# A recurrence in front of two feed-forward layers: the first chunk's instructions written in another order

## The chip, the cores and the metric

The kernel runs on one core of a Trainium2 chip. The metric is the device time of one execution in microseconds (us), the median of three timed runs. One further execution was recorded by the profiler; all rows of the profile below are from that one. TensorE is called PE (its weight loads PEld), VectorE DVE, ScalarE ACT, GpSimd POOL, and SyncE SP.

## The reference

The input has 4 batches, 8 heads, 768 tokens and a head width of 40. A gated recurrence runs over the tokens; its result goes through two gated feed-forward layers.

```python
# recurrence, per batch, head and token t
m_new = max(f + m, i)
C = exp(f + m - m_new) * C + exp(i - m_new) * outer(v, k)
n = exp(f + m - m_new) * n + exp(i - m_new) * k
y = sigmoid(o) * (C @ q) / max(|n . q|, 1)
# first layer, 320 -> 1536 -> 320
x = (sigmoid(x @ w_gate) * (x @ w_val)) @ w_out
# second layer, 320 -> 2048 -> 320
h = x @ w_in
x = (h * clip(h + 3, 0, 6) / 6) @ w_out2
```

The weights of both layers arrive as 64-bit floats; the rest is float32.

## The kernel before, in words

Tokens are cut into six chunks of 128 (`c` = 0 to 5). Inside a chunk the recurrence is written as products, batch by batch (`b` = 0 to 3), in named pieces:

- `spread` and `decays`: the forget factors of a batch are spread over all partitions by PE and scanned by DVE (L405), in two halves. For batches 2 and 3 the factors come from memory (`dec_load`).
- `scores`: q times k on PE (L379), into two PSUM banks; `weigh`: DVE multiplies each bank by the decays (L420).
- `value_ones`, `values`, `values_end`: v scaled by the input gate (`vi`) and by the last decay (`vd`), on DVE (L370) or, if "apart", as eight ACT multiplies (L368).
- `outputs`: weighed scores times `vi` on PE (L474), in pieces of 32 tokens; then the products for the state (L497), in pieces of 32 columns. For c > 0 there is also the product with the state of the chunk before (L463).
- `denominators` (L521 to L525), `gated` (y, yo: L370, L533, L540), `out_gate` (the sigmoid of o, L426, in place in the tile `vko`), `state` (ACT copies of the state, L560 and L563).
- `att2`: yo is transposed by PE (L569); ACT copies the high part of the result (L574) and DVE the low part (L575) into x.

A first-layer weight tile `raw` (three buffers) is read by ACT twice (`scaled`, L102 and L107, into `u` with one buffer and `bits` with two), joined by DVE (`to_f32`, L122), and split into a high part by ACT (`hi_in`, `hi_out1`) and a low part by DVE (`lo_in`, `lo_out1`). A job is one such tile, in the order w1 of f = 0, w1 of f = 1, wo1 of both, and so on; `work(n, ...)` takes n jobs.

The first layer of chunk c is, for each of 12 blocks f: 16 products of 512 columns (`h_pair`, L587 to L594), the sigmoid (L613), the gate multiply (L614) and the split of the result into gh and gl (L600, L601) in `m1_h`; then eight products into three banks `acc` (`m1_out`, L629 and L639), two steps later.

What sets the order: everything up to the last weight conversion of chunk 0 stands in a block under `manual_schedule`, where each engine takes its instructions in the written order. The later steps are laid out by a scheduler, steered by `quota`, `issue_after` and the calls of `work`. Each engine works through its own row in order. DMAs go out on SP's queue, also in order; a fetch of a raw tile waits there until ACT has read the tile that held the buffer.

`later_factors` makes the factors of chunks 1 to 5: a scan on DVE (L311), five small multiplies (L320), transposes (L294) and one small product (L324) on PE into three banks of the same pool `acc` that the output products use, and three ACT copies (L298 twice, L331).

Of the kernel before, what the change touches and what calls it, by code (L numbers as in the profile page):

```python
# [8 lines left out]
F32 = mybir.dt.float32  # L9
# [24 lines left out]
def mlstm_then_two_gated_ffn(  # L34
# [27 lines left out]
    def ps_acc():  # L62
        return acc_ps.tile([P, 512], F32, tag="acc", name="acc")
# [242 lines left out]
        nc.vector.memset(fz[:, 1:, 0:1], 0.0)  # L306
        nc.sync.dma_start(out=fz_dram[1:].rearrange("c r l -> r c l"), in_=fz[:, 1:, :])

    def later_factors():

        nc.vector.tensor_tensor_scan(  # L311
            out=g_sb[:, L:S], data0=fz_sb[:, L:S], data1=fs_sb[:, L:S],
            initial=0.0, op0=ALU.mult, op1=ALU.add,
        )
        transpose_rows(i_c, iT, range(1, NC), ps_acc)
        transpose_rows(g, gT, range(1, NC), ps_acc)

        ge = const.tile([BH, NC, BH // 2], F32, name="ge")
        for c in range(1, NC):
            nc.vector.tensor_scalar(  # L320
                out=ge[:, c, :], in0=sel, scalar1=g[:, c, L - 1 : L], scalar2=None, op0=ALU.mult
            )
        ps = ps_acc()
        nc.tensor.matmul(  # L324
            out=ps[:, BH // 2 : NC * BH // 2],
            lhsT=par,
            rhs=ge[:, 1:, :].rearrange("p c n -> p (c n)"),
            start=True,
            stop=True,
        )  # L330
        nc.scalar.copy(  # L331
            out=gend[:, 1:].rearrange("p c b n o -> p (c b n o)"),
            in_=ps[:, BH // 2 : NC * BH // 2],
        )

    exp_half = const.tile([P, 1], F32, name="exp_half")
    sel = const.tile([BH, BH // 2], F32, name="sel")
    odd = const.tile([BH, 2, 1], F32, name="odd")
# [105 lines left out]
    def att1(c, b, ps):  # L444

        outputs(c, b, ps)
        with tc.issue_after(last_exp[-1]):
            out_gate(c, b)
        y = denominators(c, b, state if c > 0 else None)
        gated(c, b, y, c == 1 and b < 2)  # L450
        if c == 0:
            state(c, b)

    def outputs(c, b, ps):
        a = at[c, b]
        dec, vi = a["dec"], a["vi"]

        halves = [slice(t, t + 32) for t in range(0, L, 32)]
        if c > 0:
            o_ps = a["o_ps"] = ps()  # L460
            for n in range(NP):
                for tt in halves:
                    nc.tensor.matmul(  # L463
                        out=o_ps[tt, n * 2 * D1 : (n + 1) * 2 * D1],
                        lhsT=a["qk"][:, 0, n, tt],
                        rhs=cst[:, b, n, :],
                        start=n == 0,
                        stop=n == NP - 1,
                        skip_group_check=True,
                    )  # L470
        i_ps = a["i_ps"] = ps()
        for h in range(H):
            for tt in halves:
                own = nc.tensor.matmul(  # L474
                    out=i_ps[tt, h * D1 : (h + 1) * D1],
                    lhsT=dec[:, h, tt],
                    rhs=vi[:, h, :],
                    start=h == 0,
                    stop=h == H - 1,
                    skip_group_check=True,  # L480
                )
        if c < NC - 1:
            k_on = a["vko"].rearrange("p a n -> p (a n)")[:, DM:]
            beside = c > 0
            if beside:
                c_ps = i_ps[:, H * D1 : H * D1 + NP * D1]
            else:
                c_ps = (ps() if ps is any_ps else ps_mm())[:, : NP * D1]
            c_banks[c, b] = c_ps
            with ExitStack() as queued:  # L490
                if beside:
                    queued.enter_context(tc.issue_after(own.ins))
                for h in range(H):
                    p0 = 64 * (h % 2)

                    for d in (0, 32):
                        nc.tensor.matmul(  # L497
                            out=c_ps[p0 + d : p0 + d + 32, (h // 2) * D1 : (h // 2 + 1) * D1],
                            lhsT=k_on[:, h * D + d : h * D + d + 32],
                            rhs=a["vd"][:, h, :],  # L500
                            start=not beside and h < 2,
                            stop=h >= H - 2,
                            skip_group_check=True,
                        )
# [100 lines left out]
    gs = {}  # L605
    acc1 = {}

    def m1_h(c, f, ts):
        n = ts.stop - ts.start
        banks = [ps_mm()[:, :n], ps_mm()[:, :n]]  # L610
        h_pair(slots["in", f], (1, c), banks, ts)
        g = gpool.tile([P, T], F32, tag="g", name="g")[:, :n]
        gate = nc.scalar.activation(out=g, in_=banks[0], func=AF.Sigmoid).ins  # L613
        mult = nc.vector.tensor_tensor(out=g, in0=g, in1=banks[1], op=ALU.mult).ins  # L614
        gs[c, f, ts.start] = split_g(g)
        return gate, mult

    def m1_out(c, f, ts):
        if f == 0 and ts.start == 0:
# [102 lines left out]
    with tc.manual_schedule():  # L722
        nc.sync.dma_start(out=f_sb[:, :S], in_=gates[:, 0])
        nc.scalar.dma_start(out=i_sb[:, :S], in_=gates[:, 1])
        constants()
        for b in range(2):
            qk_load(0, b)
            vko_load(0, b)
        raws = [fetch(jobs[-1][0])]
        stabilise_first()  # L730
        nc.scalar.dma_start(out=fz_dram[0], in_=fz[:, 0, :])
        for b in range(2, B):
            qk_load(0, b)
# [12 lines left out]
        value_ones(0, 0)  # L746
        next(later)
        decays(0, 0, 1)
        values(0, 0, False)
        next(second)  # L750
        scores(0, 0, any_ps)
        values_end(0, 0, True)
        decays(0, 1, 0)
        next(later)
        weigh(0, 0, 0)
        weigh(0, 0, 1)
        next(second)
        decays(0, 1, 1)
        outputs(0, 0, any_ps)
        value_ones(0, 1)  # L760
        for b in range(2):
            out_gate(0, b)
        values(0, 1, False)
        values_end(0, 1, True)
        scores(0, 1, any_ps)
        y0 = denominators(0, 0)
        gated(0, 0, y0, False)
        decays(0, 2, 0)
        weigh(0, 1, 0)
        weigh(0, 1, 1)  # L770
        outputs(0, 1, any_ps)
        state(0, 0)
        decays(0, 2, 1)
        later_decays()
        value_ones(0, 2)
        values(0, 2, False)
        y1 = denominators(0, 1)
        att2(0, 0, any_ps)
        values_end(0, 2, True)
        scores(0, 2, any_ps)  # L780
        gated(0, 1, y1, False)
        decays(0, 3, 0)
        weigh(0, 2, 0)
        weigh(0, 2, 1)
        att2(0, 1, any_ps)
        decays(0, 3, 1)
        outputs(0, 2, any_ps)
        value_ones(0, 3)
        values(0, 3, False)
        values_end(0, 3, True)  # L790
        out_gate(0, 2)
        scores(0, 3, any_ps)
        y2 = denominators(0, 2)
        u = scaled(raws[0])
        weigh(0, 3, 0)
        weigh(0, 3, 1)
        outputs(0, 3, any_ps)
        gated(0, 2, y2, False)
        out_gate(0, 3)
        x0 = to_f32(raws[0], u)  # L800
        w0 = hi_in(jobs.pop()[2], x0)
        att2(0, 2, any_ps)
        y3 = denominators(0, 3)
        gated(0, 3, y3, False)
        lo_in(w0, x0)
        opened = att2(0, 3, any_ps)
        u = scaled(raws[1])
        x1 = to_f32(raws[1], u)
        w1_ = hi_in(jobs.pop()[2], x1)
        lo_in(w1_, x1)  # L810
        for b in range(1, B):
            state(0, b)
        u = scaled(raws[2])
        x2_ = to_f32(raws[2], u)
        wo_ = hi_out1(jobs.pop()[2], x2_)
        lo_out1(wo_, x2_)

    for b in range(2):
        att_load(1, b)
        dec_load(1, b)  # L820

    halves = (0, 6)

# [93 lines left out]
    for i, (c, f, ts) in enumerate(steps):  # L917
        for _ in range(quota[i]):
            for cp, b, piece in pieces.pop(0) if pieces else ():
# [7 lines left out]
                if cp > 0 and piece == 1 and nxt[0] < NC:  # L927
# [1 line left out]
                    dec_load(*nxt)  # L929
                    qk_load(*nxt)  # L930
                    vko_load(*nxt)
        gate = m1_h(c, f, ts)
        if i == 0:
            with tc.issue_after(gate[0]), tc.issue_after(gate[1]):
                later_factors()
        outputs_but(2 if i < n_two else 1)
        before.append((c, f, ts))
        if c == 0:
            work(1 + i % 2, n_w1)
        elif c < NC - 1:  # L940

            with tc.issue_after(gate[0]):
# [198 lines left out]
```

## Time and profile before

| | us |
|---|---|
| median of three runs | 846.74 (846.21 to 846.82) |
| profiled execution | 850.12 |
| its span | 848.30 |
| PE busy in it | 825.5 (97%) |
| DVE busy | 554.2 (65%) |
| ACT busy | 424.5 (50%) |

Busy time is that of one engine alone; matmuls are pipelined, so that a record's length is longer than the distance from one start to the next. A timeline row gives start and length, and in brackets how long the engine stood idle before it and what ended that. The windows give the granted clock of TensorE: 1.00 is 2.4 GHz, 0.50 is 1.2 GHz.

### The profile page before, as it was taken

The numbers are of one execution on the slowest core, as the hardware profiler recorded it, in microseconds if no ns is written. First come the engines' busy times: TensorE is split into PE (matmuls) and PEld (weight loads), VectorE is DVE, ScalarE is ACT, GpSimd is POOL, SyncE is SP. The second block draws the span as 40 slices with busy tenths as digits, with TensorE's granted clock in tenths as the row PEclk, the third lists the DMA queues.
The fourth block names the chain that finished last, engine by engine and source line by source line (L and its number), as shares of the span: only waits on it lengthen the run. The fifth ranks groups of instructions, "written<-read, shape, count | busy, mean of one in ns | idle before, by whom it ended". The sixth has DMA issues, their size and how long they took to land.

```text
span 848.3 us, 17178 instructions
## 1 busy us (share of the span) xinstructions
PE 825.5 (97%) x7013; PEld 706.5 (83%) x7013; DVE 554.2 (65%) x995; ACT 424.5 (50%) x851; POOL 2.5 (0%) x8
## 2 busy tenths in 40 slices
PE   6789999999999999999999999999999999999998
PEld 6567889988888878888888888888998889988898
DVE  8668885875867677766755534667746577466653
ACT  5488964332534344444323535556545555365542
POOL 1000000000000000000000000000000000000000
PEclk9679999999999999999999999999999999999999
DMA  9536644332565576567404524446625466244400
GB/s 338 190 124 222 210 155 149 119 104 74 155 223 175 175 218 200 170 198 212 130 25 138 167 78 156 143 131 205 182 77 168 148 198 178 79 130 141 121 32 32
DMA packets 81423, 128.69 MB, mean 152 GB/s; under 512 B 20672, under 2 KB 57472, under 8 KB 81344
## 3 DMA queue, kind: packets, MB, share of 16 engines
q1 hardware_dynamic: 81248, 127.48, 48.9%
q8 instruction: 55, 0.90, 0.4%
q14 instruction: 24, 0.20, 0.1%
q10 hardware_dynamic: 96, 0.11, 0.0%
HBM read 104.27 MB, written 23.30 MB: 150 GB/s over the span
## 4 chain that ended last, share of the span: by engine, by line
PE 91%; DVE 5%; ACT 2%; issue 1%; DMA 0%; DVEq 0%; ACTq 0%
PE acc L629 12%; PE mm L967 9%; PE mm L591 7%; PE mm L592 7%; PE mm L593 7%; PE mm L587 5%; PE att L967 4%; PE acc L967 4%; PE acc L639 4%; PE mm L594 4%; PE att L379 3%; PE mm L1004 2%; PE mm L1006 2%; PE acc L1004 2%; PE mm L1005 2%; PE acc L1006 2%
## 5 line engine op out<-in xcount | busy, mean ns | idle before, releaser
L600 ACT CAST gh<-g 128x512 fp32r<-128x512 f32 (+1 forms) x126 | 75.7, 601 | 101.6 <-DVE g L614 71.4
L591 PE MATMUL mm<-x,w 128*128 128x512 f32 (+1 forms) x312 | 118.0, 378 | 0.0
L592 PE MATMUL mm<-x,w 128*128 128x512 f32 (+1 forms) x312 | 117.7, 377 | 0.0
L593 PE MATMUL mm<-x,w 128*128 128x512 f32 (+1 forms) x312 | 117.5, 376 | 0.0
L601 DVE TENSOR_TENSOR gl<-g,gh 128x512 fp32r<-128x512 f32 (+1 forms) x126 | 83.5, 663 | 49.8 <-ACT gh L600 49.0
L614 DVE TENSOR_TENSOR g<-g,mm 128x512 f32<-128x512 f32 (+1 forms) x78 | 50.2, 644 | 84.6 <-PE mm L594 84.1
L629 PE MATMUL acc<-gh,w 128*128 128x512 f32 (+1 forms) x312 | 103.5, 376 | 0.0
L613 ACT ACTIVATE g<-mm 128x512 f32<-128x512 f32 (+1 forms) x78 | 43.9, 563 | 93.8 <-PE mm L594 93.7
L967 PE MATMUL mm<-X,wg 128*128 128x512 f32 x336 | 84.2, 392 | 0.0
L967 PEld LDWEIGHTS mm<-X,wg 128*128 128x128 f32 x336 | 61.9, 188 | 12.8 <-DVE g L983 0.3
L592 PEld LDWEIGHTS mm<-x,w 128*128 128x128 f32 x312 | 59.4, 191 | 11.2
L593 PEld LDWEIGHTS mm<-x,w 128*128 128x128 f32 x312 | 59.4, 190 | 11.1
L629 PEld LDWEIGHTS acc<-gh,w 128*128 128x128 f32 x312 | 58.5, 190 | 10.8 <-issue 0.2
L591 PEld LDWEIGHTS mm<-x,w 128*128 128x128 f32 x312 | 59.5, 191 | 9.5
L587 PE MATMUL mm<-x,w 128*128 128x512 f32 (+1 forms) x156 | 63.9, 410 | 2.9 <-DVE w L155 1.7
L629 PE MATMUL acc<-gl,w 128*128 128x512 f32 (+1 forms) x156 | 58.8, 377 | 0.0
L982 ACT ACTIVATE gb<-c,half 128x512 f32<-128x512 f32 x48 | 34.6, 724 | 48.2 <-DVE c L978 48.2
L594 PE MATMUL mm<-x,w 128*128 128x512 f32 (+1 forms) x156 | 58.7, 376 | 0.0
L601 DVE TENSOR_TENSOR gl<-gb,gh 128x512 fp32r<-128x512 f32 x48 | 33.0, 690 | 33.8 <-ACT gh L600 33.8
L600 ACT CAST gh<-gb 128x512 fp32r<-128x512 f32 x48 | 29.5, 620 | 39.4 <-PE att L1005 39.4
L405 DVE TENSOR_TENSOR_SCAN dec<-dec,ident 128x512 f32<-128x512 f32 x40 | 47.3, 1211 | 0.0
L967 PE MATMUL att<-X,wg 128*128 128x512 f32 x168 | 46.3, 395 | 0.0
(205 smaller groups left out, 1687.3 us busy)
## 6 DMA issues: line engine op xcount, KB each, us to landing
wg<-ws_dram SPq DMA_DIRECT2D x24, 896.0 KB, 5.3
raw<-in_w SPq DMA_DIRECT2D x20, 640.0 KB, 5.3
qk<-in_qkT SPq DMA_DIRECT2D x22, 512.0 KB, 4.6
wg<-wt_dram SPq DMA_DIRECT2D x48, 224.0 KB, 6.0
vko<-in_vko SPq DMA_DIRECT2D x22, 480.0 KB, 6.3
dec<-fz_dram SPq DMA_DIRECT2D x20, 512.0 KB, 5.0
raw<-in_wo SPq DMA_DIRECT2D x14, 640.0 KB, 3.9
X<-xt_dram SPq DMA_DIRECT2D x84, 64.0 KB, 3.1
```

The lines of the kernel that those rows point to most:

```text
L405: nc.vector.tensor_tensor_scan(out=x, data0=a["factors"][n] if "factors" in a else x, data1=ident4.rearrange("p h l -> p (h l)"), initial= ...
L587: nc.tensor.matmul(out=banks[j], lhsT=tail, rhs=xl[:, 2, :], start=True, stop=False)
L591: nc.tensor.matmul(out=banks[j], lhsT=hi, rhs=xh[:, k, :], start=False, stop=False)
L592: nc.tensor.matmul(out=banks[j], lhsT=hi, rhs=xl[:, k, :], start=False, stop=False)
L593: nc.tensor.matmul(out=banks[j], lhsT=lo, rhs=xh[:, k, :], start=False, stop=False)
L594: nc.tensor.matmul(out=banks[j], lhsT=tail, rhs=xh[:, 2, :], start=False, stop=True)
L600: nc.scalar.copy(out=gh, in_=g)
L601: nc.vector.tensor_tensor(out=gl, in0=g, in1=gh.bitcast(F32), op=ALU.subtract)
L613: gate = nc.scalar.activation(out=g, in_=banks[0], func=AF.Sigmoid).ins
L614: mult = nc.vector.tensor_tensor(out=g, in0=g, in1=banks[1], op=ALU.mult).ins
L629: nc.tensor.matmul(out=a[m], lhsT=lhsT, rhs=rhs, start=st and lhsT is hi and rhs is gh, stop=en and lhsT is lo, skip_group_check=True,)
L967: nc.tensor.matmul(out=ps, lhsT=w[:, a, s, :], rhs=x[:, b, :], start=first and i == 0, stop=i == 3, skip_group_check=True,)
```

## The change

The pieces of the recurrence of chunk 0 are written in another order, and some work is moved into that block:

- Raw weights are read by ACT earlier (`scaled(raws[0])` ahead of `outputs(0, 0)`, `scaled(raws[1])` after `att2(0, 1)`), with the fetch of the next raw tile, and the loads of chunk 1 (`att_tiles`, `qk_load`, `vko_load`, `dec_load`), called right behind.
- The sigmoids of batches 2 and 3 and the state copies of batches 1 to 3 stand earlier; `decays(0, 2, 1)` and `later_decays` stand ahead of `weigh(0, 1)`; `scores(0, 3)` ahead of `outputs(0, 2)`; `values_end(0, 3)` goes from ACT to DVE.
- For c = 0, `outputs` takes all 128 tokens in one product per head, and its state products 64 columns.
- Two h blocks (f = 0 and 1) and their gates are written in the block. `later_factors` is cut in three (`later_scan`, `later_ends`, the rest), placed around them.
- For chunk 1, `gated` of batches 0 and 1 scales y on DVE, no longer on ACT.
- `work(1 + i % 2)` becomes `work(2 - i % 2)`.

PE in the block, from the work of batch 1 up to the first h block. `dec`, `early` are decays, `vi`, `vd` scaled values, `yo` the gated output, `x` and `w` the operands of the first layer. Before:

```order
L569 MATMUL acc<-ident_81,yo 128x128 x3
L379 MATMUL att<-early 128x128 x8
L569 MATMUL mm<-ident_81,yo 128x128 x3
L474 MATMUL mm<-vi,early 32x41 x32
L497 MATMUL mm<-vd,early 32x41 x16
L379 MATMUL acc<-early 128x128 x8
L474 MATMUL acc<-vi,early 32x41 x32
L497 MATMUL att<-vd,early 32x41 x16
L569 MATMUL att<-ident_81,yo 128x128 x3
L294 MATMUL acc<-ident_81,early 128x32 x5
L379 MATMUL att<-qk 128x128 x4
L569 MATMUL mm<-ident_81,yo 128x128 x3
```

The change:

```order
L504 MATMUL acc<-vd,vko 64x41 x8
L384 MATMUL att<-early 128x128 x8
L576 MATMUL mm<-ident_81,yo 128x128 x3
L384 MATMUL mm<-early 128x128 x8
L480 MATMUL acc<-vi,early 128x41 x8
L504 MATMUL acc<-vd,early 64x41 x8
L480 MATMUL acc<-vi,early 128x41 x8
L504 MATMUL att<-vd,early 64x41 x8
L576 MATMUL att<-ident_81,yo 128x128 x3
L576 MATMUL mm<-ident_81,yo 128x128 x3
L384 MATMUL att<-qk 128x128 x7
```

`scores` of batch 3 (the second 128x128 x8) goes ahead of `outputs` of batch 2, the pieces become 8 products each, the transposes of `later_factors` (128x32) leave this place, and most scores of chunk 1 (`att<-qk`) stand behind both transposes of yo.

DVE, from y of batch 2 to the low part of x that h0 waits for (`den`: denominators, `bits`: a joined weight, L151 and L155 the low part of the first weight). Before:

```order
L370 TENSOR_TENSOR y<-mm,den 128x8x40
L533 TENSOR_TENSOR yo<-y,early 128x320
L122 SCALAR_TENSOR_TENSOR bits<-u,bits 128x640
L575 TENSOR_TENSOR x<-att,x 128x3x128
L521 TENSOR_SCALAR den<-acc 128x8
L524 TENSOR_TENSOR den<-den,acc 128x8
L525 RECIPROCAL den<-den 128x8
L370 TENSOR_TENSOR y<-acc,den 128x8x40
L533 TENSOR_TENSOR yo<-y,early 128x320
L151 TENSOR_TENSOR w<-bits,w 128x2x256
L155 TENSOR_TENSOR w<-bits,w 64x128 x2
L575 TENSOR_TENSOR x<-mm,x 128x3x128
```

The change:

```order
L375 TENSOR_TENSOR y<-acc,den 128x8x40
L540 TENSOR_TENSOR yo<-y,early 128x320
L528 TENSOR_SCALAR den<-acc 128x8
L531 TENSOR_TENSOR den<-den,acc 128x8
L532 RECIPROCAL den<-den 128x8
L375 TENSOR_TENSOR y<-acc,den 128x8x40
L540 TENSOR_TENSOR yo<-y,early 128x320
L582 TENSOR_TENSOR x<-att,x 128x3x128
L151 TENSOR_TENSOR w<-bits,w 128x2x256
L155 TENSOR_TENSOR w<-bits,w 64x128 x2
L582 TENSOR_TENSOR x<-mm,x 128x3x128
```

The joined weight (L122) is gone from here, it stands further up; the denominators of batch 3 stand ahead of the low part of x of batch 2.

ACT around the first two gates (`g`, `gh`; `cst` are the state copies, `iT`, `gT`, `gend` the factors of later chunks). Before:

```order
L560 COPY cst_86<-acc 104x164
L613 ACTIVATE g<-mm 128x512
L563 COPY cst<-cst_86 40x4x41 x2
L560 COPY cst_86<-mm 104x164
L298 COPY iT<-acc 128x160
L563 COPY cst<-cst_86 40x4x41 x2
L560 COPY cst_86<-att 104x164
L600 CAST gh<-g 128x512
L563 COPY cst<-cst_86 40x4x41 x2
L102 ACTIVATE u<-raw 128x640
```

The change:

```order
L624 ACTIVATE g<-mm 128x512
L102 ACTIVATE u<-raw 128x640
L107 ACTIVATE bits<-raw 128x640 x2
L607 CAST gh<-g 128x512
L165 CAST w<-bits 128x2x320
L624 ACTIVATE g<-mm 128x512
L102 ACTIVATE u<-raw 128x640
L607 CAST gh<-g 128x512
L298 COPY iT<-acc 128x160
L298 COPY gT<-acc 128x160
L335 COPY gend<-acc 128x80
```

The state copies are gone from between the gates; a weight's high part (L165) stands between gh of f = 0 and the second sigmoid, and the three copies of `later_factors` stand behind gh of f = 1.

The diff, cut to its core:

```diff
-        gated(c, b, y, c == 1 and b < 2)
+        gated(c, b, y, False)
...
-        halves = [slice(t, t + 32) for t in range(0, L, 32)]
+        m = 32 if c > 0 else L
+        halves = [slice(t, t + m) for t in range(0, L, m)]
...
-                    for d in (0, 32):
+                    m = 32 if beside else 64
+                    for d in range(0, 64, m):
...
         decays(0, 1, 1)
+        u0 = scaled(raws[0])
+        fetched.append(fetch(jobs[-4][0]))
+        att_tiles(1, 0)
+        qk_load(1, 0)
         outputs(0, 0, any_ps)
...
         gated(0, 0, y0, False)
+        vko_load(1, 0)
         decays(0, 2, 0)
+        decays(0, 2, 1)
+        later_decays()
         weigh(0, 1, 0)
         weigh(0, 1, 1)
+        att_tiles(1, 1)
+        qk_load(1, 1)
+        state(0, 0)
+        att2(0, 0, any_ps)
         outputs(0, 1, any_ps)
-        state(0, 0)
-        decays(0, 2, 1)
-        later_decays()
         value_ones(0, 2)
+        for b in range(2, B):
+            out_gate(0, b)
...
+        x0 = to_f32(raws[0], u0)
+        y1 = denominators(0, 1)
         gated(0, 1, y1, False)
+        vko_load(1, 1)
+        w0 = hi_in(jobs.pop()[2], x0)
...
         att2(0, 1, any_ps)
+        u1 = scaled(raws[1])
+        fetched.append(fetch(jobs[-4][0]))
+        for b in range(2):
+            dec_load(1, b)
+        scores(0, 3, any_ps)
         decays(0, 3, 1)
         outputs(0, 2, any_ps)
         value_ones(0, 3)
+        state(0, 1)
         values(0, 3, False)
-        values_end(0, 3, True)
-        out_gate(0, 2)
-        scores(0, 3, any_ps)
-        y2 = denominators(0, 2)
-        u = scaled(raws[0])
+        values_end(0, 3, False)
+        state(0, 2)
         weigh(0, 3, 0)
         weigh(0, 3, 1)
+        y2 = denominators(0, 2)
+        gated(0, 2, y2, False)
         outputs(0, 3, any_ps)
...
+        first_h = m1_products(0, 0, slice(0, T))
+        x1 = to_f32(raws[1], u1)
+        state(0, 3)
         w1_ = hi_in(jobs.pop()[2], x1)
+        later_scan()
         lo_in(w1_, x1)
-        for b in range(1, B):
-            state(0, b)
-        u = scaled(raws[2])
-        x2_ = to_f32(raws[2], u)
+        second_h = m1_products(0, 1, slice(0, T))
+        opened = m1_sigmoid(first_h)
+        u2 = scaled(raws[2])
+        fetched.append(fetch(jobs[-4][0]))
+        first_gate = m1_gate(0, 0, slice(0, T), first_h, opened)
+        later_ends()
+        x2_ = to_f32(raws[2], u2)
         wo_ = hi_out1(jobs.pop()[2], x2_)
+        second_gate = m1_gate(0, 1, slice(0, T), second_h)
         lo_out1(wo_, x2_)
-
-    for b in range(2):
-        att_load(1, b)
-        dec_load(1, b)
+        later_factors()
...
-        gate = m1_h(c, f, ts)
-        if i == 0:
-            with tc.issue_after(gate[0]), tc.issue_after(gate[1]):
-                later_factors()
+        gate = (first_gate, second_gate)[i] if i < 2 else m1_h(c, f, ts)
...
-            work(1 + i % 2, n_w1)
+            work(2 - i % 2, n_w1)
```

## Rows read from the trace of the kernel before

**Rows 1.** The page's first part: busy us (share of the span), xinstructions.

```profile
PE 825.5 (97%) x7013; PEld 706.5 (83%) x7013; DVE 554.2 (65%) x995; ACT 424.5 (50%) x851; POOL 2.5 (0%) x8
```

**Rows 2.** PE's waits, 100 us to the end: us in total, times, longest.

```profile
PE acc L1004 <- ACT gh L600: 0.9, 2, 0.5
...
PE mm L1004 <- ACT gh L600: 0.5, 1, 0.5
```

**Rows 3.** Windows: us, busy of PE, PEld, DVE, ACT, POOL, granted clock, DMA, GB/s.

```profile
45.00:47.00 2.00, 2.00 (x6) 1.52 (x5) 1.27 (x3) 1.23 (x4) 0.00 (x0) 0.50 0.79 307
...
86.00:88.00 2.00, 2.00 (x6) 1.52 (x6) 2.00 (x4) 1.89 (x6) 0.00 (x0) 0.50 0.82 296
```

**Rows 4.** PE's timeline, 43 to 85 us: start, us, operation [idle before, releaser].

```profile
43.22 0.79 PE L587 MATMUL mm<-x,w 128*128 128x512 f32 x1 [1.16 <-DVE x L575]
...
45.09 0.63 PE L591 MATMUL mm<-x,w 128*128 128x512 f32 x1
...
45.52 0.63 PE L592 MATMUL mm<-x,w 128*128 128x512 f32 x1
...
55.07 0.49 PE L294 MATMUL acc<-ident,early 32*128 32x32 f32 x5 [1.05 <-DVE early L311]
...
57.15 0.44 PE L324 MATMUL acc<-ge,par 32*128 32x80 f32 x2 [1.58 <-DVE ge L320]
...
61.97 0.40 PE L587 MATMUL mm<-x,w 128*128 128x512 f32 x1
...
62.20 0.40 PE L591 MATMUL mm<-x,w 128*128 128x512 f32 x1
...
84.73 0.50 PE L587 MATMUL mm<-x,w 128*128 128x512 f32 x1 [1.33 <-DVE w L155]
```

**Rows 5.** PE's timeline, 5 to 38 us.

```profile
5.33 2.04 PE L279 MATMUL mm<-early,ident 32*128 32x128 f32 x8 [5.33 <-ACT early L246]
...
20.65 1.28 PE L474 MATMUL acc<-vi,dec 128*32 128x41 f32 x56 [0.23 <-DVE dec L420]
...
35.98 0.49 PE L497 MATMUL att<-vd,early 128*32 128x41 f32 x14 [1.50 <-issue]
...
37.24 0.74 PE L294 MATMUL acc<-ident,early 32*128 32x32 f32 x5
```

**Rows 6.** DVE's timeline, 16 to 41 us.

```profile
16.57 0.16 DVE L521 TENSOR_SCALAR den<-att 128x8 f32<-128x8 f32 x1
...
17.20 0.49 DVE L370 TENSOR_TENSOR y<-att,den 128x320 f32<-128x320 f32 x1
...
17.79 0.49 DVE L533 TENSOR_TENSOR yo<-y,vko 128x320 f32<-128x320 f32 x1
...
25.26 1.22 DVE L405 TENSOR_TENSOR_SCAN early<-early,ident 128x512 f32<-128x512 f32 x1
...
26.40 1.26 DVE L420 TENSOR_TENSOR early<-att,early 128x512 f32<-128x512 f32 x2
...
27.58 0.55 DVE L575 TENSOR_TENSOR x<-mm,x 128x384 fp32r<-128x384 f32 x1
...
31.56 1.29 DVE L420 TENSOR_TENSOR early<-acc,early 128x512 f32<-128x512 f32 x2 [1.41 <-PE acc L379]
...
38.54 0.56 DVE L575 TENSOR_TENSOR x<-att,x 128x384 fp32r<-128x384 f32 x1 [3.96 <-ACT x L574]
...
40.16 0.49 DVE L533 TENSOR_TENSOR yo<-y,early 128x320 f32<-128x320 f32 x1
```

**Rows 7.** ACT's timeline at 36.5 us.

```profile
36.52 0.47 ACT L426 ACTIVATE early<-early 128x320 f32<-128x320 f32 x1 [2.40 <-PE att L497]
```

**Rows 8.** SP's queue at 3.15 us; DMA issues: xcount, KB, median us to landing.

```profile
3.15 0.43 SPq L95 DMA_DIRECT2D raw<-in_w  x1
...
raw<-in_w SPq DMA_DIRECT2D x12, 640.0 KB, 3.9
```

More of the change, by code (lines that the diff above doesn't have):

```diff
@@ L307, in later_decays, with later_scan @@
         nc.sync.dma_start(out=fz_dram[1:].rearrange("c r l -> r c l"), in_=fz[:, 1:, :])
-    def later_factors():
+    def later_scan():
         nc.vector.tensor_tensor_scan(
@@ L314, in later_factors, with later_ends @@
         )
-        transpose_rows(i_c, iT, range(1, NC), ps_acc)
-        transpose_rows(g, gT, range(1, NC), ps_acc)
-        ge = const.tile([BH, NC, BH // 2], F32, name="ge")
+    def later_ends():
         for c in range(1, NC):
@@ L322, in later_factors @@
             )
+    def later_factors():
+        transpose_rows(i_c, iT, range(1, NC), ps_acc)
+        transpose_rows(g, gT, range(1, NC), ps_acc)
         ps = ps_acc()
@@ L334, in later_factors @@
         )
+    ge = const.tile([BH, NC, BH // 2], F32, name="ge")
     exp_half = const.tile([P, 1], F32, name="exp_half")
@@ L494, in outputs @@
                     p0 = 64 * (h % 2)
-                    for d in (0, 32):
+                    m = 32 if beside else 64
+                    for d in range(0, 64, m):
                         nc.tensor.matmul(
-                            out=c_ps[p0 + d : p0 + d + 32, (h // 2) * D1 : (h // 2 + 1) * D1],
-                            lhsT=k_on[:, h * D + d : h * D + d + 32],
+                            out=c_ps[p0 + d : p0 + d + m, (h // 2) * D1 : (h // 2 + 1) * D1],
+                            lhsT=k_on[:, h * D + d : h * D + d + m],
                             rhs=a["vd"][:, h, :],
@@ L606, in mlstm_then_two_gated_ffn, with m1_products @@
     acc1 = {}
-    def m1_h(c, f, ts):
+    def m1_products(c, f, ts):
         n = ts.stop - ts.start
@@ L611, in m1_h, with m1_sigmoid, m1_gate @@
         h_pair(slots["in", f], (1, c), banks, ts)
+        return banks
+    def m1_sigmoid(banks):
+        n = banks[0].shape[-1]
         g = gpool.tile([P, T], F32, tag="g", name="g")[:, :n]
-        gate = nc.scalar.activation(out=g, in_=banks[0], func=AF.Sigmoid).ins
+        return g, nc.scalar.activation(out=g, in_=banks[0], func=AF.Sigmoid).ins
+    def m1_gate(c, f, ts, banks, opened=None):
+        g, gate = opened or m1_sigmoid(banks)
         mult = nc.vector.tensor_tensor(out=g, in0=g, in1=banks[1], op=ALU.mult).ins
@@ L616, in m1_h @@
         return gate, mult
+    def m1_h(c, f, ts):
+        return m1_gate(c, f, ts, m1_products(c, f, ts))
     def m1_out(c, f, ts):
@@ L767, in mlstm_then_two_gated_ffn @@
         gated(0, 0, y0, False)
+        vko_load(1, 0)
         decays(0, 2, 0)
+        decays(0, 2, 1)
+        later_decays()
         weigh(0, 1, 0)
         weigh(0, 1, 1)
+        att_tiles(1, 1)
+        qk_load(1, 1)
+        state(0, 0)
+        att2(0, 0, any_ps)
         outputs(0, 1, any_ps)
-        state(0, 0)
-        decays(0, 2, 1)
-        later_decays()
         value_ones(0, 2)
+        for b in range(2, B):
+            out_gate(0, b)
         values(0, 2, False)
-        y1 = denominators(0, 1)
-        att2(0, 0, any_ps)
         values_end(0, 2, True)
         scores(0, 2, any_ps)
+        x0 = to_f32(raws[0], u0)
+        y1 = denominators(0, 1)
         gated(0, 1, y1, False)
+        vko_load(1, 1)
+        w0 = hi_in(jobs.pop()[2], x0)
         decays(0, 3, 0)
@@ L788, in mlstm_then_two_gated_ffn @@
         value_ones(0, 3)
+        state(0, 1)
         values(0, 3, False)
-        values_end(0, 3, True)
-        out_gate(0, 2)
-        scores(0, 3, any_ps)
-        y2 = denominators(0, 2)
-        u = scaled(raws[0])
+        values_end(0, 3, False)
+        state(0, 2)
         weigh(0, 3, 0)
         weigh(0, 3, 1)
+        y2 = denominators(0, 2)
+        gated(0, 2, y2, False)
         outputs(0, 3, any_ps)
[L798 to L802, printed above, removed]
         y3 = denominators(0, 3)
         gated(0, 3, y3, False)
+        att2(0, 2, any_ps)
         lo_in(w0, x0)
-        opened = att2(0, 3, any_ps)
-        u = scaled(raws[1])
-        x1 = to_f32(raws[1], u)
+        att2(0, 3, any_ps)
+        first_h = m1_products(0, 0, slice(0, T))
+        x1 = to_f32(raws[1], u1)
+        state(0, 3)
         w1_ = hi_in(jobs.pop()[2], x1)
+        later_scan()
         lo_in(w1_, x1)
-        for b in range(1, B):
-            state(0, b)
-        u = scaled(raws[2])
-        x2_ = to_f32(raws[2], u)
+        second_h = m1_products(0, 1, slice(0, T))
[5 more added lines that the diff above has]
+        x2_ = to_f32(raws[2], u2)
         wo_ = hi_out1(jobs.pop()[2], x2_)
+        second_gate = m1_gate(0, 1, slice(0, T), second_h)
         lo_out1(wo_, x2_)
-    for b in range(2):
-        att_load(1, b)
-        dec_load(1, b)
+        later_factors()
     halves = (0, 6)
```

## The prediction

> **What bounds the kernel now.** Of the page, the share of busy time comes first: PE is busy 97% of the span [rows 1], so only the remaining few per cent and the slow stretches can be had. The list of PE's waits from 100 us to the end says where they are not: three waits, 1.4 us together [rows 2]. The loss lies ahead of 100 us, and PE's timeline there gives five stretches. A, to 43.22 us: the recurrence of chunk 0, until the first h block (16 products of 512 columns, called h0, h1, ... in the order of f) may start. B, to 52.7: h0 and h1. C, to 61.97, where h2 starts: products of `later_factors` and the first output products, between waits of 1.05 and 1.58 us [rows 4]. D, from h2 to h6 at 84.73, which begins with PE's last long wait, 1.33 us [rows 4]. E, from there to the end.
>
> The clock is read from the windows: 45 to 47 us and 86 to 88 us were granted 0.50, the lower level of 1.2 GHz [rows 3]. Neighbouring 512-column products start 0.43 us apart there (45.09, 45.52) and 0.23 at the full rate (61.97, 62.20) [rows 4]. Each of the two followed a stretch in which PE had waited. After h6 some 8 products ran at the lower level, 8 x 0.20 = 1.65 us.
>
> On all engines the rows behind h6 stand in the same order before and after. So the change is worth the difference in h6's start, and whether slow products follow it. I worked A to D out by laying the new order of PE, DVE and ACT down row by row, each instruction starting when its engine is free and its inputs are there (0.04 us for a signal), with durations from rows. Done so for the old order, h0 comes at 42.8 and h6 at 84.2, where the trace has 43.22 and 84.73: the method is good to half a microsecond here.
>
> **The change, part by part.**
>
> 128-token outputs. Before, `outputs` of a batch is 32 products of 32 tokens, 64 records, 1.28 us for the last 56 [rows 5]: 0.07 us for four, which run side by side on four column groups. Now it is 8 products, 16 records, each with all 128 columns of weights, one after the other. No row shows 128 weight columns with 41 moving ones. Below: the load hides, 16 x 0.068 = 1.1 us. Above: as in the 32x128 products, 8 records in 2.04 us, 0.255 each [rows 5], 4.1 us. Nearest are the transposes with 128 weight columns and 32 moving ones: (0.74 - 0.26) / 4 = 0.12 each [rows 5]. I take 0.123 x 16 = 1.97 us, that is 0.8 us more than now for each batch. For the 64-token state products I keep 0.8 us (now 0.7).
>
> TensorE: Matmul & The Clock Gate of the Trainium skill (section Packing small matmuls) says that a weight load overlaps running products only when the row groups differ; here every load uses all rows. The 512-column products contradict that as a general rule: they start 0.43 us apart at 1.2 GHz, no more than 512 columns need, so their loads hide. The same page (section LDWEIGHTS) has 128 columns at 107 ns; by load plus stream, an estimate, `outputs` would take 16 x 0.175 = 2.8 us.
>
> Stage A. `outputs(0,0)` starts at 14.94 as before and ends at 16.9; the three small operations (0.63), y (0.59) and yo [rows 6], which waits for the sigmoids behind the earlier weight reads on ACT, end at 19.0 (18.3 before). Both scans of batch 2 now stand ahead of `weigh(0,1)`: 2 x 1.14 + 0.25 [rows 6], then 1.2, so 22.8 (20.6 before). `outputs(0,1)` to 24.8, beside 1.6 us of DVE's x, vi and bits; y and yo to 26.4; scan 1.14; `weigh(0,2)` to 28.8 (27.6 before) [rows 6]. From here it turns. `scores(0,3)` stands ahead of `outputs(0,2)`, so DVE runs x, scan, vi and the new vd product (0.47, taken from ACT's eight multiplies) straight into `weigh(0,3)`, which ends at 32.7, as now (31.56 + 1.2) [rows 6]. PE has `outputs(0,2)` from 30.4, `outputs(0,3)` from 33.2 to 35.2, and den follows at once. Before, PE stops for 1.50 us in the last state products [rows 5]; the sigmoid waits 2.40 us for them [rows 7], behind it on ACT stand the high halves of the first weight and the cast of x, DVE waits 3.96 us for that [rows 6], and den of batch 3 stands behind it on DVE. Now the sigmoids are far ahead, and den before x. yo of batch 3 ends at 36.8 (40.6 before) [rows 6]. Transposes, low halves of w and x follow to 39.9. h0 starts at 39.9: **3.3 us earlier**.
>
> The raw reads moved into A: 1.4 us on ACT at 14.3, in front of the table load and sigmoids. They need a tile issued at 3.15; raw tiles land in 3.9 us [rows 8], so 7 us of slack. The fourth raw fetch stands ahead of batch 0's q and k of chunk 1 on SP's queue and shifts those by one 640 KB tile; they are used at 38 us. Were this cover gone, h0 would slip by the lateness. The state copies, before in B and C on ACT, now stand in its waits in A: 3 x 0.95 us.
>
> Stage B is 10 slow and 22 fast products both times, 9.5 us: ends 49.4.
>
> Stage C. The scan of `later_factors` now runs in B, where DVE waits for h0. Left on PE: transposes 0.8, the small product 0.3, then a wait: output banks are those of `later_factors`, released by three copies on ACT that stand behind gh of f = 1. That gives 52.2, 1.6 us idle. Ten products, half of them slow, 3.7 us: h2 at 55.9. C takes 6.5 instead of 9.25: **2.8 us**.
>
> Stage D. Four h blocks 14.6, 15 output products 3.4 (12 before), recurrence of chunk 1 3.2, and waits for the low halves of weight 4 (1.1), for yo of chunk 1 (0.8) and 0.15: 23.45 instead of 22.75, **0.7 us lost**. The weights of f = 3, 5, 7 are converted a step earlier; the y scaling of two batches leaves ACT (8 multiplies) for DVE (0.5).
>
> h6 at 79.4: 5.35 us earlier. E: the wait ahead of it is under 1 us, so I expect no slow products: 1.65. Sum 7.0. The profiled execution took 850.12 for a span of 848.30; the runs' median is 846.74, 3.4 less. The 1.50 us stall has no releaser, and may be the profiled execution's alone; I count half of it, 0.75 less. **846.74 - 7.0 + 0.75 = 840.5 us.**
>
> **Rivals.**
>
> (1) Loads in series: 0.12 plus 0.068 a record (the skill's rule above comes to the same mechanism). The four `outputs` are all on the path, 64 records x 0.065 = 4.2 us of the gain lost: 844.7. For it: nothing hides a load on the same rows in the small transposes; against: the 512-column pitch.
>
> (2) ACT and DVE are the bound in D. Between 60 and 90 us conversions, gates and chunk 1 share both, and PE's 1.33 us wait is for a converted weight [rows 4]. Starting 6 us sooner, PE could find each weight later than I put it: two waits 0.8 longer, with slow products behind one of them (1.65) as after 84.73: 7.0 - 3.25, or 843.7. Against: the old order is laid down rightly by the same rows.
>
> (3) Loads hidden fully: 2.1 us more, 838.4.
>
> (4) Slower: the 128-column records cost what the 32x128 products do, 0.255, in A. Four batches x 16 x 0.132 = 8.4 us, and 2.0 for the state products at half of that gain: 850.9. It turns from faster to slower at 0.22 to 0.23 a record. Against: those have 128 moving columns, not 41.
>
> (5) Nothing moves: the sum would have to hide in E, where PE waits 1.4 us in all [rows 2]; no row speaks for it.
>
> **How the numbers follow.** Forecast 0.55, (1) 0.13, (2) 0.16, (3) 0.09, (4) 0.04, (5) 0.03. The range 837.0 to 845.0 takes in (1), (2) and (3). A measurement of this kernel can tell 0.2% from no change, 1.7 us: faster needs under 845.05. The forecast, (3) and nearly all of (1) and (2) are below it: 0.87; same 0.08; slower 0.05.
>
> **What would show it.** Right: PE's first 512-column product near 40 us, h2 near 56, h6 near 79.5, granted clock 1.00 behind it; `outputs` rows of chunk 0 of about 2 us; no DVE wait of 4 us for a cast of x; a wait of 1 to 2 us for `gend` before the first output product. Wrong: `outputs` of 3 us or more; PE waits above 1.3 us between 60 and 80 with a granted clock of 0.50 behind them; or an h6 that is 5 us earlier and a span that is not.

## The result, and the profile after

The changed kernel takes 853.51 us (median of 4 runs, 851.85 to 855.13) where the kernel before takes 846.78 beside it: ratio 1.0074, with an interval of 1.0060 to 1.0089. It is slower by 6.7 us; 840.5 had been predicted. The profiled execution took 851.85 us for a span of 850.0.

The share of busy time has risen, which here is no gain (PE was at 97% [rows 1]): a weight load that takes long counts as busy.

```profile
PE 833.1 (98%) x6757; PEld 714.9 (84%) x6757; DVE 555.5 (65%) x998; ACT 419.0 (49%) x827; POOL 2.5 (0%) x8
```

PE's waits from 0 to 110 us: in total, times, longest. The two waits for an h block's x and w and the two of `later_factors` [rows 4] are gone; in their place stand one for the copy of iT, which had been forecast at 1.6, and a pause that nothing releases.

```profile
PE mm L279 <- ACT early L246: 5.3, 1, 5.3
PE acc L646 <- issue: 3.1, 1, 3.1
PE acc L646 <- ACT iT L298: 1.4, 1, 1.4
PE acc L480 <- DVE dec L425: 0.9, 1, 0.9
```

PE's timeline at the places of [rows 4 and 5]: start, busy time, operation.

```profile
10.88 2.08 PE L384 MATMUL acc<-qk 40*128 40x128 f32 x16
...
14.89 3.64 PE L480 MATMUL att<-vi,dec 128*128 128x41 f32 x16
18.45 1.08 PE L504 MATMUL mm<-vd,vko 128*64 128x41 f32 x16
19.46 2.08 PE L384 MATMUL mm<-qk 40*128 40x128 f32 x16
...
23.76 3.81 PE L480 MATMUL acc<-vi,dec 128*128 128x41 f32 x16 [0.90 <-DVE dec L425]
27.50 1.08 PE L504 MATMUL acc<-vd,vko 128*64 128x41 f32 x16
...
47.05 0.79 PE L594 MATMUL mm<-x,w 128*128 128x512 f32 x1
47.64 0.63 PE L598 MATMUL mm<-x,w 128*128 128x512 f32 x1
48.07 0.63 PE L599 MATMUL mm<-x,w 128*128 128x512 f32 x1
...
55.88 0.81 PE L294 MATMUL acc<-ident,early 32*128 32x32 f32 x10
...
58.79 0.50 PE L646 MATMUL acc<-gh,w 128*128 128x512 f32 x1 [1.42 <-ACT iT L298]
...
62.09 0.63 PE L594 MATMUL mm<-x,w 128*128 128x512 f32 x1
...
75.21 0.39 PE L646 MATMUL acc<-gh,w 128*128 128x512 f32 x1 [3.09 <-issue]
...
87.09 0.50 PE L594 MATMUL mm<-x,w 128*128 128x512 f32 x1
87.43 0.40 PE L598 MATMUL mm<-x,w 128*128 128x512 f32 x1
87.67 0.40 PE L599 MATMUL mm<-x,w 128*128 128x512 f32 x1
```

`outputs` of a batch (L480) occupies PE from 14.89 to 18.45: 3.56 us for 16 records, 0.223 each, where 0.123 had been taken. The four batches take 3.56, 3.74, 3.56 and 3.57, 14.4 us in all against 7.9. The 64-column state products (L504) take 1.01 each against 0.8. So h0 starts at 47.05, which is 3.8 us later than before [rows 4], not 3.3 earlier; h2 at 62.09 (61.97 before); h6 at 87.09 (84.73 before), with products 0.23 to 0.24 us apart behind it.

PE's weight loads in the same stretch say what the records wait for.

```profile
12.89 1.77 PEld L279 LDWEIGHTS att<-early,ident 32*128 32x128 f32 x8 [0.22 <-issue]
14.88 3.49 PEld L480 LDWEIGHTS att<-vi,dec 128*128 128x128 f32 x16 [0.22 <-issue]
18.45 0.94 PEld L504 LDWEIGHTS mm<-vd,vko 128*64 128x64 f32 x16
19.46 1.78 PEld L384 LDWEIGHTS mm<-qk 40*128 40x128 f32 x16
```

The loads of `outputs` fill 3.49 of its 3.6 us: the load unit works without a gap and is the bound, 0.218 us a load. That is the price of L279's loads (1.77 / 8 = 0.22), which also fill 128 columns, though with 32 rows and 128 moving columns. The scores (L384) have 128 columns too and pay half, 0.11: their heads sit in turn on rows 0 and 64 of the array.

On DVE, den now waits for these products, and the 3.96 us wait for ACT's cast [rows 6] has shrunk to 0.70, as forecast.

```profile
27.61 0.17 DVE L528 TENSOR_SCALAR den<-acc 128x8 f32<-128x8 f32 x1 [1.70 <-PE acc L480]
...
41.61 0.17 DVE L528 TENSOR_SCALAR den<-acc 128x8 f32<-128x8 f32 x1 [2.92 <-PE acc L480]
...
43.97 0.56 DVE L582 TENSOR_TENSOR x<-att,x 128x384 fp32r<-128x384 f32 x1 [0.70 <-ACT x L581]
...
45.76 0.56 DVE L582 TENSOR_TENSOR x<-mm,x 128x384 fp32r<-128x384 f32 x1
```

The last step before h0 is another one, which the forecast had not. x is ready at 46.32, but scores of chunk 1 stand ahead of h0 on PE, and these have waited for ACT's copy of the last state:

```profile
45.05 2.07 PE L384 MATMUL att<-qk 40*128 40x128 f32 x14 [0.77 <-ACT cst L567]
```

So h0 starts 0.7 us later than x would have let it.

### The profile page after: what moved, and what is told of

Same layout as the page of the kernel before. It is cut to its first block, busy times and chain, and to the rows that moved or that the text cites. A ratio compares the mean times of both kernels' runs of the same rounds, so it can differ in the third digit from the quotient of the medians.

```text
span 850.0 us, 16640 instructions
## 1 busy us (share of the span) xinstructions
PE 833.1 (98%) x6757; PEld 714.9 (84%) x6757; DVE 555.5 (65%) x998; ACT 419.0 (49%) x827; POOL 2.5 (0%) x8
## 4 chain that ended last, share of the span: by engine, by line
PE 90%; DVE 6%; ACT 2%; issue 1%; DMA 0%; DVEq 0%; ACTq 0%
PE acc L646 11%; PE mm L997 9%; PE mm L598 7%; PE mm L599 7%; PE mm L600 7%; PE mm L594 4%; PE att L997 4%; PE acc L997 4%; PE acc L656 4%; PE mm L601 4%; PE att L384 3%; PE mm L1034 2%; PE acc L1034 2%; PE mm L1036 2%; PE mm L1035 2%; PE acc L1035 2%
```

## The experiments

Theory P: the new order gains what was forecast, and the price of the wide records eats it. Theory O: the order itself loses. Edits are to the changed kernel unless the kernel before is named.

**Column widths.** Outputs and states both back to 32 columns:

```diff
-        m = 32 if c > 0 else L
+        m = 32
-                    m = 32 if beside else 64
+                    m = 32
```

> The changed kernel with chunk 0's products back in pieces: 32-token outputs and 32-column state products; the new order kept. Theory P (the price of the 128-column records): in the changed kernel each outputs of chunk 0 takes 3.64 us and each set of state products 1.08, in the kernel before about 1.28 and 0.77; four batches, nearly all on the path. With pieces h0 should start at 37.5 to 39 us (47.05 in the changed kernel, 43.22 before) and the time should be 841 to 845 us. Theory O (the new order itself loses it, by waits in the later stages and stalls of PE's instruction stream): h0 earlier, but the time stays at 849 or more.

846.0 us, ratio 0.9978 (0.9966 to 0.9991): above P's range and below O's. h0 starts at 38.12, as P expected. Its profile has two pauses that nothing releases; O had named such stalls, but as a loss of the new order, and the kernel before has one too [rows 5]. They are taken up below.

```profile
34.27 0.35 PE L504 MATMUL att<-vd,early 128*32 128x41 f32 x14 [1.09 <-issue]
...
67.13 0.59 PE L646 MATMUL acc<-gh,w 128*128 128x512 f32 x1 [2.87 <-issue]
```

The outputs alone back to 32 tokens, the 64-column states kept (first line of that diff):

> The changed kernel with 32-token outputs alone; the 64-column state products stay. Theory P: the outputs carry the loss, the state products at most 0.3 us a batch: within 1.5 us of the kernel with both in pieces, 841 to 846 us. Theory O: 849 or more.

842.52 us, ratio 0.9941 (0.9921 to 0.9960): 5.0 us faster than the kernel before (3.4 to 6.7) and 11 faster than the change. PE's timeline:

```profile
29.09 1.32 PE L480 MATMUL acc<-vi,early 128*32 128x41 f32 x64
...
38.68 0.79 PE L594 MATMUL mm<-x,w 128*128 128x512 f32 x1
```

h0 starts at 38.68 instead of 47.05. Those 8.4 us come from one line: the four batches of short records take 1.25, 1.72, 1.25 and 1.59 us (short waits included), 5.8 in all instead of 14.4, and 0.2 comes back as a wait for yo. O falls: with this one line undone, the rest of the change gains.

64-token outputs (`m = 32 if c > 0 else 64`):

> The changed kernel with 64-token outputs, 16 products, 32 records in two column groups. If a record's time is that of loading its weight columns (128 columns 0.22 us), a 64-column load takes 0.11, and two groups load side by side: about 0.063 a record as in the 64-column state products of the changed kernel (16 in 1.08), 2.0 us a batch; h0 near 41, time 844 to 848 us. If records of different column groups don't load side by side: as the changed kernel, 851 to 855.

844.5 us, ratio 0.9964 (0.9951 to 0.9977), as expected for two column groups that load side by side; 32 records in 1.94 us, h0 at 39.68, h2 at 54.87, h6 at 79.39:

```profile
14.72 1.94 PE L480 MATMUL att<-vi,dec 128*64 128x41 f32 x32
...
39.68 0.79 PE L594 MATMUL mm<-x,w 128*128 128x512 f32 x1
...
54.87 0.40 PE L594 MATMUL mm<-x,w 128*128 128x512 f32 x1
...
79.39 0.50 PE L594 MATMUL mm<-x,w 128*128 128x512 f32 x1
```

A batch costs 1.3, 1.9 and 3.6 us with 32, 64 and 128 columns, so the loss grows steeply between 64 and 128.

The other way round, the kernel before with the 128-token outputs alone:

```diff
-        halves = [slice(t, t + 32) for t in range(0, L, 32)]
+        m = 32 if c > 0 else L
+        halves = [slice(t, t + m) for t in range(0, L, m)]
```

> The kernel before with 128-token outputs for chunk 0 as the only change. Theory P: four times 2.4 us, all on the path there: h0 near 52 us, time 854 to 858 us. Theory O: within 2 us of the kernel before (846.8).

857.52 us, ratio 1.0112 (1.0092 to 1.0132): 9.5 us slower, as P expected. h0 starts at 50.16 instead of 43.22; that it does not come near 52 may be put down for the most part to the pause of 1.50 us [rows 5], which this profile has not.

```profile
22.36 3.81 PE L475 MATMUL acc<-vi,dec 128*128 128x41 f32 x16 [1.20 <-DVE dec L420]
...
50.16 0.79 PE L588 MATMUL mm<-x,w 128*128 128x512 f32 x1 [1.16 <-DVE x L576]
```

The kernel before with the 64-column states alone (`m = 64 if not beside else 32`, and d over `range(0, 64, m)`):

> The kernel before with one part of the change alone, the state products of the first chunk in 64-column records (16 a batch instead of 32). Price theory: 16 records 1.06 us instead of 32 in 0.77, four times, is 1.1 to 1.2 us more, of which the pause of 1.50 at 34.5 to 36.0 us may be given back, since 64 records fewer stand ahead of it: median 845.5 to 848.5 (before 846.8). If the pause stays, 847.5 to 848.5; if it goes, 845.5 to 847. The rival, that the 64-column states are what the change lost by (3 us or more in place of 1.2): 849 or more.

849.71 us, ratio 1.0016 (1.0002 to 1.0029), 0.2 to 2.5 us slower. Four times 16 records in 1.08 instead of 32 in 0.77 is 1.2. The median lies above the range given and, as it stands, in that of the rival; but the kernel before took 847.94 beside it, not 846.8, and the interval of the ratio leaves out a loss of 3 us. So the rival falls and a loss of 1.2 fits, no more: the profile, a single one, had no pause and a span 1.2 us shorter than before's, where the price theory then expected no loss.

**What makes the record dear.** Twice the moving columns:

```diff
-                    rhs=vi[:, h, :],
+                    rhs=vi[:, h0 : h0 + wide, :].rearrange("p h d -> p (h d)"),
```

> The changed kernel with 82 instead of 41 moving columns in each of the first chunk's output products (two heads' values; the first chunk's outputs are then not the reference's). Theory W (loading the 128 columns of weights sets the price of 0.223 us, the moving columns pass beside the next load): 16 records stay at 3.6 to 3.8 us, the product of the first feed-forward block starts at 47 to 48 us. Theory S (load and moving columns in series): the 41 further columns add 0.07 to 0.1 us a record (as 82 against 41 columns do in the later chunks' 32-column records, 0.78 us for 32 against 0.79 for 64), 16 records take 4.7 to 5.3 us, and the first product starts at 51 to 54 us.

One run, 852.9 us. W holds: 41 more columns cost 0.07 us in 16 records, and h0 starts at 47.00.

```profile
14.54 3.71 PE L482 MATMUL att<-vi,dec 128*128 128x82 f32 x16
```

A quarter of the rows (`lhsT=dec[: 32 if c == 0 else P, h, tt]`, and vi likewise):

> The changed kernel with the first chunk's output products over 32 of the 128 source tokens only (the first chunk's outputs are then not the reference's): 128 columns of weights as before, 32 rows in place of 128. The transposes from which the prediction took 0.12 us a record have 32 rows. If the rows of the weight tile make the difference: 16 records take 1.9 to 2.2 us and the first product starts at 40 to 42 us. If the 128 columns of a two-pass record cost 0.22 us whatever the rows: 16 records stay at 3.5 to 3.7 us and the first product at 46.5 to 47.5 us.

One run, 851.56 us. The rows make no difference:

```profile
33.05 3.63 PE L480 MATMUL acc<-vi,early 32*128 32x41 f32 x16
```

That agrees with the Trainium skill (TensorE: Matmul & The Clock Gate, section Step-by-step: what each phase is for): the time of a weight load scales with the count of columns, not of rows.

128-token outputs in all chunks (`m = L`):

> The changed kernel with 128-token output records in all six chunks, not in the first alone: 8 of 82 and 16 of 41 moving columns a batch in place of 32 and 64. It reads the price of a 128-column record where the products run 0.23 us apart. If the price goes with TensorE's clock: 0.11 to 0.13 us a record, 24 records in 2.7 to 3.1 us against 1.4 now, 20 batches, 25 to 35 us more: 877 to 888. If it is the same 0.22 us at both clocks: 24 records in 5.3 us, 75 to 85 us more: 925 to 940.

One run, 875.42 us, just under the range for a price that goes with the clock. In chunk 1, where products run 0.23 us apart, the same 16 records take half:

```profile
71.35 1.87 PE L480 MATMUL att<-vi,dec 128*128 128x41 f32 x16
```

0.117 us there against 0.223 in chunk 0. TensorE therefore ran chunk 0 of the changed kernel at the lower level (1.2 GHz), and the products behind it still start 0.43 us apart, although the window reads a granted clock of 1.00:

```profile
47.00:49.00 2.00, 2.00 (x6) 1.57 (x6) 2.00 (x3) 1.11 (x3) 0.00 (x0) 1.00 0.00 0
```

That is an inference from the distances, but the kernel before bears it out: its scores take 2.08 us in a stretch that was granted 0.50, and the same 2.08 at 10.93 us, where the window reads 1.00. The first change of the clock that its trace records comes at 23.9 us (49.9 in the changed kernel); ahead of that the reading doesn't tell the clock here.

```profile
10.93 2.08 PE L379 MATMUL acc<-qk 40*128 40x128 f32 x16
...
29.38 2.08 PE L379 MATMUL acc<-early 40*128 40x128 f32 x16
...
29.00:31.00 2.00, 2.00 (x42) 1.91 (x34) 1.08 (x5) 1.28 (x6) 0.00 (x0) 0.50 0.84 213
```

**The pause without a releaser.** It was not that of one execution: the changed kernel, a_wide82 and a_rows32, whose PE stream has the same number of records, all have it behind record 468 (3.09, 1.72 and 2.97 us), right after a burst of short records. To move the count, extra products on ident stand ahead of the first transposes, while PE is idle:

```diff
+            for k in range(160 if b == 0 and n == 0 else 0):
+                tt = slice(32 * (k % 4), 32 * (k % 4) + 32)
+                nc.tensor.matmul(out=ps[tt, :32], lhsT=ident[:, tt], rhs=ident[:, :32], ...)
```

> The changed kernel with 160 extra TensorE records of 32 columns, ahead of the first transposes, in the 5.28 us in which TensorE stands idle at the start (their results are overwritten). It moves the place in TensorE's instruction stream at which the 3.09 us pause with no releaser stood (after about 469 records, at 72.2 to 75.2 us, right behind 192 short records in 1.7 us). Theory C (the pause comes at a fixed count of instructions, and is long only where a burst of short records ends there): at 72 to 75 us no pause over 0.3 us, since the count is reached some 10 us earlier among 512-column products; the profiled span is 2 to 3.5 us shorter than the changed kernel's 850.0, the median 848.5 to 851. Theory B (the burst alone makes it, wherever it stands): the pause of 2.5 to 3.5 us stays behind the same burst, the median 851.5 to 855. On the side: if the 128-column records are dear because TensorE's clock is low in this stretch, early work may raise it, and the 16 output records at 15 us take less than 3.0 us instead of 3.64; if not, they stay at 3.6.

855.94 us (ratio 1.0089, 1.0057 to 1.0122), outside both ranges: each product is two records, so there were 320, and the pause came among them:

```profile
1.35 3.21 PE L279 MATMUL mm<-ident 128*32 128x32 f32 x223 [1.35 <-POOL ident masks.py:199]
8.49 1.51 PE L279 MATMUL mm<-ident 128*32 128x32 f32 x97 [3.92 <-issue]
```

It cost more than it saved (the transposes start 4.65 us late), but behind the burst at 75 us no pause is left. B, that the burst alone makes it, is ruled out. The outputs stay at 3.64 us, so this early work did not raise the clock. With 78 products (156 records):

> The changed kernel with 78 extra 32-column products (156 records) in the idle time at the start, few enough to end by 3.6 us, before the first transposes at 5.3 us. Theory C (the pause without a releaser falls where TensorE's records reach a count of about 219, 470, 721 or 975, and is long when a burst of short records ends there): these counts now fall among 512-column products or ahead of the bursts, so no pause over 0.5 us up to 110 us, the first product still starts at 47 to 47.5 us, and the profiled span is 846 to 848.5 instead of 850.0, the median 848 to 851.5. Theory B (the burst of records alone makes it): the pause of 1.5 to 3.5 us stands behind the batch's outputs at 72 us as before; median 851.5 to 855.

850.79 us, ratio 1.0028 (1.0016 to 1.0039), as C expected, with no pause up to 110 us and none behind the burst:

```profile
72.28 0.48 PE L510 MATMUL att<-vd,vko 128*32 128x41 f32 x30
72.69 0.50 PE L652 MATMUL acc<-gh,w 128*128 128x512 f32 x1
```

The span fell by 1.1 us only, just under the 1.5 to 4 expected, and h6 comes at 86.36 instead of 87.09: between h2 and h6 PE now has five waits, 2.1 us together, for DVE's w (0.61 and 0.39), ACT's g (0.42) and yo (0.28 and 0.41). The first of w and that of g stand at 66 and 69 us, ahead of the place of the pause, and a_rows32 has them beside its pause, so the pause had not hidden these two.

**Better versions.** The 32-column outputs and states, with these 156 records:

> The order of the changed kernel with 32-token outputs and 32-column state products (as the run before of that kind, 846.0 us, with pauses of 1.09 at 33 and 2.87 at 64 to 67 us), and the same 156 extra records at the start. Theory C: the pause of 2.87 goes, since its count now falls 30 records ahead of that burst; the one of 1.09 may come back at another batch; median 841 to 843.5. Theory B: both pauses stay, 845 to 847.

841.68 us, ratio 0.9914 (0.9892 to 0.9935). The pause of 2.87 is gone; two shorter ones stand in chunk 0, one of them behind record 602, a count that C had not named:

```profile
27.95 0.59 PE L486 MATMUL acc<-vi,early 128*32 128x41 f32 x40 [0.41 <-issue]
...
32.58 0.41 PE L486 MATMUL acc<-vi,early 128*32 128x41 f32 x9 [0.78 <-issue]
...
38.46 0.79 PE L600 MATMUL mm<-x,w 128*128 128x512 f32 x1
```

And a_out32 with `later_factors()` moved up behind `later_ends()`:

> The fastest version so far (the changed kernel with 32-token outputs, 842.5 us, in which TensorE waits 1.42 us for ACT's copy of the later chunks' gates) with later_factors called right after later_ends, ahead of the third weight tile's work, so that its three copies stand earlier on ACT. If that wait is what ends last there: the third feed-forward block starts 1.0 to 1.4 us earlier than 53.7 us, median 841 to 842. If the low half of the third weight tile or the second gate is late next: 842 to 843.5, with a wait of 0.8 to 1.5 us for DVE's w or ACT's gh in its place.

842.52 us, ratio 0.9927 (0.9905 to 0.9949). The wait for iT is gone; 0.59 us for ACT's w and 0.95 for DVE's w take its place, which is the second case:

```profile
51.27 0.50 PE L594 MATMUL mm<-x,w 128*128 128x512 f32 x1 [0.95 <-DVE w L155]
```

h2 starts 2.4 us earlier than 53.71, more than either case had, but products behind it run 0.43 us apart again and output products follow, and h3 comes at 58.82 instead of 57.79: the time is that of a_out32. These last two and a_out32 beat both kernels, and can't be told from one another.

## Why the prediction was wrong

**The step that failed** is the price of a 128-column output record: "I take 0.123 x 16 = 1.97 us". It is 0.223 to 0.234, so four batches cost 14.4 us instead of 7.9 (6.5 more); the state products at 1.01 instead of 0.8 add 0.85. Together 7.4, and h0 came 7.15 us after the forecast 39.9. "`outputs` of 3 us or more" was among the prediction's own signs of being wrong. The run with 64-token outputs pays the price that the forecast took (1.94 us a batch against 1.97), and its h0 is at 39.68: with that price the rest of stage A comes out right in sum. In part that is luck: the states cost 0.85 more than taken and the scores of chunk 1, which the forecast left out, 0.7 (x is ready at 38.93 there), so that the other terms were as much too long.

The 0.123 came from transposes, chosen because their 32 moving columns were nearest to 41. Moving columns were the wrong measure: 41 or 82 take 3.64 or 3.71 us, and with 32 rows it is 3.63. What sets the price is the load of 128 columns, and the right row was the one used as the upper bound, L279 [rows 5], set aside for its 128 moving columns. From its start at 5.33 [rows 5] to the next row of the trace before, its 8 records cost 0.23 each:

```profile
7.17 0.26 PE L294 MATMUL mm<-ident,early 32*128 32x32 f32 x1
```

Why a transpose's load is cheaper at the same width was not tried. The rule of the Trainium skill that the prediction argued against (TensorE: Matmul & The Clock Gate, section Packing small matmuls: loads overlap running products only where the row groups differ) is borne out so far as the scores, in turn on two row groups, pay 0.11 a load; no run varied that alone. But 64-column records on the same rows, in turn on two column groups, cost 0.06 and not half of 0.22, so that column groups count as well. The same page's 107 ns for a load of 128 columns (section LDWEIGHTS) is half of the 0.218 measured in chunk 0, and the measurement decides; the 0.117 a record in chunk 1 of the run with wide outputs everywhere is near it.

**Rival (4)** was this mechanism, at 0.255 us a record, with the turn from faster to slower at 0.22 to 0.23. That turn leaves out the state products which the same rival counts with 2.0 us for 8.4; with them, 6.2 us of gain are used up at 0.20 (6.2 / 1.24 / 64 above 0.123), and the measured 0.223 lies beyond it. Its chance of 0.04 was the second mistake: both ends of a bound of 0.068 to 0.255 were open, and the middle was taken because it looked alike.

**The other terms.** B took 8.8 us (9.5 forecast). C took 6.2 (6.5), with its wait of 1.42 (1.6). D took 25.0 (23.45), of which 3.09 is the pause; without it 21.9. E: no slow products stand behind h6, as forecast, but of 1.65 only 0.66 is left (850.0 - 87.09 against 848.30 - 84.73), since PE waits at 118.83 us for DVE's x:

```profile
118.83 0.50 PE L594 MATMUL mm<-x,w 128*128 128x512 f32 x1 [0.61 <-DVE x L582]
```

What the other 0.4 went into was not followed. In sum, against the 843.1 forecast for a profiled execution: 7.15 - 0.7 - 0.3 + 1.55 + 1.0 = 8.7, and 851.85 was measured. The median lies 4.3 us further from its forecast: the profiled execution of before was 3.4 above its median and that of after 1.7 below, less the 0.75 that the forecast had added back for half of the stall.

Three sums of the prediction are off without changing the outcome: D's terms add up to 23.25 and not 23.45; rival (3) would be 3.5 us by the path that (1) takes, not 2.1; and the 1.28 us for 56 short records are 0.09 for four, not 0.07.

**The order itself** gains, as theory P says, and the change lost by the width of its records. How much it gains is less sure. With 64-token outputs, at the price that was forecast, h0, h2 and h6 start at 39.68, 54.87 and 79.39 against 39.9, 55.9 and 79.4 (B and C 0.8 short and D 1.1 long, two errors that cancel), and the span is 6.0 us below before's. But its median is only 3.0 us below that of the kernel before (1.9 to 4.2), where 6.2 had been forecast: the losses were read in one execution that took 3.4 us more than the median, and nearly all of them were then taken off the median. With 32-column pieces and the long pause moved away, 0.9914 of before is 7.3 us (5.5 to 9.2). The forecast's 7.0 had paid 0.8 a batch for wide outputs and 0.1 for wide states; without these its terms give 10.6, which no run reached.

Left open: the changed kernel's four runs are two pairs, 851.9 and 855.1. A second pause would be of that size, but no profile caught the longer one.

## What to carry to other kernels

Price a small product by the weight-load rows, not by the product rows: by the columns that it loads, the clock of that stretch and, as far as the scores here show it, whether the next load goes to the same rows; a few wide loads can cost three times as much as many narrow ones that lie side by side. Where a price is bounded from 0.068 to 0.255 and decides the sign, work out the turning point and take the row with the same kind of load, not the same stream. A gap that nothing releases may hang on the count of instructions: look for the same count in other kernels, and for an instruction transfer just ahead of its end, before calling it chance. And take a loss off the median only if it stands in more than one execution.

## What the runs showed of the hardware

Every pause of PE without a releaser stands at one of few counts of PE's records: 223; 468 (three kernels), 473 (two) and 475; 602; 724; 1487 (two); 1614 and 1615; 1743. They lie about 126 records, or multiples of it, apart: 250 from 223 to 473, 127 from 475 to 602, 122 on to 724, 763 on to 1487, 127 on to 1614, 129 on to 1743. The page of the changed kernel lists instruction transfers of 0.87 MB in 53 packets, 16.4 KB each, one for 255 of PE's products and loads (2 x 6757 in all); the kernel before has 55 for 2 x 7013, 255 again.

```profile
q8 instruction: 53, 0.87, 0.4%
```

The Trainium skill (Runtime: NRT & Kernel Launch, section Instruction fetch mechanics) says that an engine's instructions are refilled in blocks of 16 KiB, 256 instructions, and that crossing one is mostly hidden. The spacing fits that (126 products and 126 loads are 252); "mostly hidden" holds for most blocks, but a crossing cost from 0.3 to 3.9 us where it showed. The transfers' own times go further than the counts. These packets come some 16 us apart on average, yet each of the 14 pauses ends 1.28 to 1.60 us after one has landed. In the changed kernel PE stands idle from 72.13 us, the packet moves from 72.78 to 73.71, and PE goes on at 75.21:

```profile
q8 instruction: 1, 0.02, 5.3%
```

(The view is that of 72.7 to 73.8 us.) So PE waits for the refill, as far as timing can show it; no run changed the refill alone. A burst shortens the time that is left for it: the 126 records ahead of the pause at 75.21 took 1.7 us. But that does not suffice, since in the kernel before they took 5.7; what makes a packet start late was not found.
